# An adaLN transformer block on one core: softmax reciprocals moved from VectorE to GpSimd, and the last chunk's MLP weights requested round by round

## The chip, the cores and the metric

The kernel runs on one core of a Trainium2 chip. A core has a matrix engine (TensorE, "PE" in the profile, with its weight loads as "PEld"), VectorE ("DVE"), ScalarE ("ACT"), GpSimd ("POOL"), and SyncE ("SP"), which here only issues DMA transfers. Each engine works through its own list of instructions in order, and waits at semaphores for the others. The metric is the time of one execution in microseconds (us) on the device. The kernel before took 804.7 us, the median of 3 runs (804.57 to 805.7).

## The reference

The computation is one block with adaptive layer norm, self-attention and a bilinear gated MLP. The input x is (1, 2048, 640) in bf16; there are 32 heads of 20; the MLP's inner width is 1536.

```python
mod = (_silu(c) @ w_mod).reshape(1, 6, 1, -1)
sa, ca, ga, sb, cb, gb = (mod[:, i] for i in range(6))
h = layernorm(x) * (1 + ca) + sa
q, k, v = split_heads(h @ wqkv)                # 32 heads of 20
p = softmax(q @ k.T * 20 ** -0.5)              # 2048 x 2048 for each head
x = x + ga * ((p @ v) @ wo)
h = layernorm(x) * (1 + cb) + sb
x = x + gb * (((h @ w_gate) * (h @ w_up)) @ w_down)
```

## The kernel before, in words

**Order.** The file does not write out the order of its instructions. It describes every instruction as a task (class `Task`, line 39) with an engine, a planned duration, what it depends on, and a priority, and a list scheduler (class `Sched`, line 131) plays the whole program through once while the kernel is built. The order in which tasks start in that play is the order of each engine's list; `emit_program` (line 350) writes the lists with their semaphore waits. So a changed constant (`PE_SWITCH`, `PV_W`, `HAM_MIN`, `FILL_HARD`, or an entry of the table `STAGE`, which replaces such constants from a given item on) changes no computation, but may move any instruction. At run time nothing is rearranged: an engine that waits at one instruction also holds back all that stands behind it in its list. DMA transfers from SP have the same property: SP issues them one behind the other, in list order.

**Chunks and items.** The 2048 queries are taken in six chunks (512, 512, 256, 256, 256, 256). For a chunk, the 32 heads come in eight sets of four (`NSET`), and one set in one chunk is an item. For an item, PE computes transposed scores, four heads in the four 32-row strips of the array (line 1511), into PSUM; each group of scores fills two banks of it. ACT takes exp of the two banks at once (line 1548, 128x1024). Two pairs of banks alternate, so ACT can be at most a group behind PE. For a part of the groups' neighbours ("quads") DVE and POOL compute exp in place of ACT with integer operations: lines 1572, 1604 and 1612 on DVE, and a product that is either four quarter pieces on POOL (line 1624) or one whole operation on DVE (line 1609). PE then multiplies the exponentials with V (line 2177); V has a column of ones in front, so the same matmuls give the softmax denominators.

**End of an item** (`item_end_tasks`, line 1694). T1: DVE transposes the result out of PSUM into `OT` (line 1704). T2: DVE takes the reciprocals of the denominators into `invT` (line 1709). T3: `OTn` = `OT` times `invT` (line 1711), on POOL, or on DVE for the last set of heads of a chunk. T4: DVE transposes back into `OcT` (line 1720). Then four or five small DMA copies on SP move the rows into `Ocp` (line 1732), which the output projection reads.

**Behind each chunk** (`suffix`, line 1759). The output projection with its residual, the second layer norm (lines 1830 to 1837; its power of −1/2 is POOL's line 1835), transposes (line 1853 for the last chunk), twelve rounds of gate and up projection (one for each 128 of the 1536 columns), their product, the down projection, and the second residual (line 2047) are interleaved with the attention of the chunk that follows. Matmuls of this part are issued in quarters of the array (`quarters`, line 959, whose instruction is line 961); those of the last chunk, behind which no attention follows, use the whole array (`full`, line 957).

**MLP weights.** For each round, one load for gate and one for up (160 KB each, line 1917, on SP). Chunks before the last use the three buffers `stg` in turn: a pair can be asked for once the round three before it is done. The last chunk, number 5, finds ten of its twelve pairs in buffers of their own, `stx`, in which no other chunk's weights stand, and only its last two pairs go through `stg`. The dependency that decides from when on the `stx` pairs may be asked for stands in one expression:

```python
(sfx_done["qdead"] if fc < nsq else first)
    + oc_ready[(NC - 2, CHUNKS[-2][1] // 128 - 1)]   # if use_x
```

Here `fc` is the pair, `sfx_done["qdead"]` and `first` say when the memory that the buffers reuse is free, and `oc_ready[...]` are the `Ocp` copies of the last item of chunk 4.

Of the kernel before, what the change touches and what calls it, by code (L numbers as in the profile page):

```python
# [7 lines left out]
ALU = mybir.AluOpType  # L8
AX = mybir.AxisListType
BF16 = mybir.dt.bfloat16  # L10
F32 = mybir.dt.float32
# [1 line left out]

SEM = 60.0
PE_DRAIN = 170.0
PE_SWITCH = 102.0
PE_BACK = 112.0
PV_W = 219.0
X_FIRST = 0.0
ACT_LAT = 250.0  # L20
DVE_LAT = 40.0
# [10 lines left out]
STEAL_END = 66197.894  # L32
STEAL_GAP = 200
HAM_W = 3413.3
HAM_MIN = 2550.0
LKTOL = 300.0


# [311 lines left out]
def emit_program(nc, sched, nsem_dma=56):  # L350
# [123 lines left out]
CHUNKS = ((0, 512), (512, 512), (1024, 256), (1280, 256), (1536, 256), (1792, 256))  # L474
# [6 lines left out]
PV_KEEP = 2  # L481
# [10 lines left out]
EAGER = 7  # L492
# [3 lines left out]
XBACK = 0  # L496
HOLD = 110
PVTOL = 249
XDPRIO = 1.343
TPRIO = 0.75  # L500
TAHEAD = 1
GU_ONE = 1
XCONT = 0
T3_POOL = 1
HEAD_OUT = 2
NPS = 4
TS_4X, TT_2X = 600.0, 1145.0
# [23 lines left out]
PV0N = 1  # L531
GATE_F = (0.446, 0.6, 0.5, 0.5, 0.5, 1.0)
FILL_MIN = 4190.746
FILL_HARD = 3000.0
FILL_T0, FILL_TH, FILL_MINH = 2300.0, 17000.0, 7500.0
FILL_MODE = 'P'
DUP_MIN = 0.0
# [17 lines left out]
NTERM = 2  # L555

STAGE = {
    0: {"D_LATE": 16, "PVMIN": 2, "X_LATE": -179.96, "XDPRIO": 1.343, "LKTOL": 300.0, "FILL_MIN": 4190.746, "HOLD": 95, "TPRIO": 0.75, "PVTOL": 249, "EAGER": 9, "X_HALF": 0.0, "XBACK": 0, "D_RES": 74, "PVCAP": 12, "PVMAX": 14, "STEAL_GAP": 200, "PV_KEEP": 2},
    2: {"DL": 0.376},
    4: {"HOLD": 53.4},  # L560
    5: {"HOLD": 88.7, "STEAL_GAP": 176.5},
    7: {"DL": 0.501},
    9: {"LKTOL": 115.1},
    10: {"X_HALF": 5.8},
    11: {"DL": 0.443, "EAGER": 4, "FILL_MIN": 3731.3, "X_HALF": 38.6},
    12: {"DL": 0.459, "LKTOL": 438.4, "STEAL_GAP": 303.4, "EAGER": 10, "X_HALF": 21.8},
    13: {"DL": 0.417, "FILL_MIN": 4496.3, "STEAL_GAP": 266.2, "X_HALF": 20.9},
    15: {"LKTOL": 166.0, "PVMAX": 5, "EAGER": 10, "XBACK": 1},
    16: {"PVCAP": 10, "PVMAX": 3, "EAGER": 10, "FILL_MIN": 5086.4},
    17: {"X_HALF": -35.2},  # L570
    18: {"EAGER": 3, "X_LATE": -36.1, "HOLD": 42.4, "PVMIN": 1},
    19: {"DL": 0.471, "EAGER": 2, "X_HALF": 94.7},
    20: {"DL": 0.391},
    21: {"EAGER": 6, "FILL_MIN": 4510.3, "X_HALF": 24.2, "D_LATE": 5},
    22: {"PVMAX": 7, "X_HALF": 147.8, "EAGER": 9, "X_LATE": -21.9, "HOLD": 66.8},
    23: {"HOLD": 124.7, "X_HALF": 14.5},
    24: {"DL": 0.464},
    25: {"DL": 0.549, "PV_KEEP": 3, "X_LATE": 36.2},
    26: {"DL": 0.411, "X_LATE": 65.8, "PVMAX": 3, "EAGER": 8},
    27: {"DL": 0.473, "XBACK": 1, "HOLD": 186.0, "FILL_MIN": 3881.8, "X_LATE": -1.8},  # L580
    28: {"X_HALF": 33.6, "FILL_MIN": 4310.0, "XBACK": 0},
    29: {"PVMAX": 7, "X_LATE": -9.2},
    30: {"X_LATE": -109.9, "HOLD": 140.4, "XBACK": 1},
    31: {"X_LATE": 202.7, "D_RES": 21},
    32: {"PVCAP": 11, "X_HALF": -25.7, "X_LATE": 197.5},
    33: {"DL": 0.442},
    34: {"PVMIN": 5, "X_HALF": 27.8, "XBACK": 1},
    35: {"X_HALF": -31.6, "PVMAX": 14},
    36: {"DL": 0.524},
    37: {"X_LATE": -50.4},  # L590
    40: {"XBACK": 1, "HOLD": 36.3},
    41: {"X_LATE": 52.1, "X_HALF": -52.1},
    44: {"X_LATE": -66.5, "EAGER": 4, "D_RES": 10},
    47: {"FILL_MIN": 5302.0},
    48: {"PVCAP": 14, "FILL_MIN": 3192.3},
}
XHALF = 1
STG_G0, STG_G, XC_G = 12, -10, -20
# [12 lines left out]
def build_kernel(nc, A_x, A_wqkv, A_wo, B_x, B_w_gate, B_w_up, B_w_down, c, w_mod, out):  # L611
# [195 lines left out]
    def dve(dur, f, deps=(), prio=3.0, **k):  # L807
        return sc.add(Task("dve", dur, f, deps, prio=prio, **k))
# [73 lines left out]
    def load_rest():  # L882
# [5 lines left out]
        for q, f in enumerate((first2[0], first2[1],  # L888
# [690 lines left out]
    for qi, (it, us) in enumerate(dquads):  # L1579
# [36 lines left out]
        if X_POOL and qi % X_POOL == X_POOL - 1 and qi < len(dquads) - X_LAST and all(  # L1616
                dquads[z][0] == it for z in range(qi, min(len(dquads), qi + X_TAIL + 1))):
            st_["xby"] = None
            for x in range(X_PIECES):
                w = 2048 // X_PIECES  # L1620

                def fxp(e, x=x, w=w, st_=st_):
                    d = DSl[st_["ss"][0]][:, x * w:x * w + w].bitcast(BF16)
                    return e.tensor_tensor(d, DBl[st_["slot"]][:, x * w:x * w + w].bitcast(BF16), d, ALU.mult)  # L1624
                t = Task("pool", w * POOL_NS + 180.0, fxp, [tm, te], prio=2.0 + .1 * qi + .01 * x, name=f"XP.{qi}")
                t.lk = 2
                t.cond = lambda st_=st_: st_["xby"] != "dve"

                def on_p(task, x=x, st_=st_):
# [17 lines left out]
            def on_x(task, o0=o0, st_=st_):  # L1647
# [46 lines left out]
    def item_end_tasks(it):  # L1694
        ci, j = items[it]
        if ci == NC - 1 and j == 0:
# [12 lines left out]
        t2 = dve(155, lambda e: e.reciprocal(invT[:, 0:nb32].unsqueeze(2),  # L1709
                                            OT[:, 0:n].rearrange("p (b c) -> p b c", c=32)[:, :, 0:1]), [t1], prio=pe_)  # L1710
        f3 = lambda e: e.tensor_tensor(  # L1711
            OTn[:, 0:n].rearrange("p (b c r) -> p b r c", c=32, r=2),
            OT[:, 0:n].rearrange("p (b r c) -> p b r c", c=32, r=2),
            invT[:, 0:nb32].rearrange("p (b r) -> p b r", r=2).unsqueeze(3).to_broadcast([128, nb32 // 2, 2, 32]), ALU.mult)
        direct = j == NSET - 1 and ci == NC - 1
        if T3_POOL and not direct and not (END3 and j == NSET - 1):
            t3 = pool(n * 2.2 + 200, f3, [t2], prio=0)
        else:
            t3 = dvl(sb_cost(n, 1.04), f3, [t2], prio=pe_)
# [39 lines left out]
    def suffix(ci):  # L1759
# [148 lines left out]
        for fc in range(FT):  # L1908
            use_x = tail and fc < nsx
            wbuf, dm = [], []  # L1910
            for w_, wv in enumerate((wgv, wuv)):
                cell = {}
                if use_x:
                    cell["t"] = stx[fc][:, w_, :, :]

                def f(e, wv=wv, fc=fc, cell=cell):
                    return e.dma_start(cell["t"], wv[:, :, fc * 128:(fc + 1) * 128])
                t = dma("sp", int(STG_B * 128 * KD * 128 * 2), f,
                        (sfx_done["qdead"] if fc < nsq else first) + oc_ready[(NC - 2, CHUNKS[-2][1] // 128 - 1)] if use_x else
                        kp_use if ci == 0 else [], prio=16 + ci + .01 * fc,  # L1920
                        gate=int(gstart[NC] - 40) if tail and not use_x else 0 if tail else max(0, gb + (STG_G0 if ci == 0 else STG_G)))
                if not use_x:
                    t.acq = [(sStg[w_], "s", 1)]

                    def on0(task, cell=cell, w_=w_):
                        cell["i"] = task.slots["s"]
                        cell["t"] = stg[cell["i"]][:, w_, :, :]
                    t.on_start = on0
                wbuf.append(cell)
                dm.append(t)  # L1930
# [102 lines left out]
        for tl in range(ntl):  # L2033
# [5 lines left out]
            for (c_, w) in cuts:  # L2039
# [10 lines left out]
                if tail and TAILX:  # L2050
# [535 lines left out]
```

## Time and profile before

| what | us |
|---|---|
| median of 3 runs | 804.7 (804.57 to 805.7) |
| the profiled execution | 806.1 |
| its span, first to last instruction | 804.3 |
| PE busy | 786.4 |
| ACT busy, of it exps | 762.8, 746.8 |
| DVE busy | 688.5 |
| POOL busy | 361.9 |
| end of the last exp | 775.85 |

The profile is one execution of its own, with its own time. "Busy" is the time in which an engine executes something; busy times of engines overlap. In a row of groups the columns are: line of the kernel, engine, operation, tile written and tiles read, shape and type of each, count; then busy us and mean ns of one; then the idle time of the engine just ahead of such instructions and what ended it. In a row of a timeline they are: start in us from the span's start, duration of the run of like instructions in us, engine and line, operation, tiles, shape, count, and in brackets the idle time before it with its releaser. The releaser is inferred from semaphores: where an instruction waited for several things, the row names the one that seemed last, which can be wrong. A table by stretches gives busy us (and instructions) of PE, PEld, DVE, ACT and POOL, then the granted PE clock as a share of full speed, the busy share of the DMA engines, and GB/s.

### The profile page before, as it was taken

The page shows a single profiled execution, that of the slowest core. Times are in us where ns is not written, and L with a number is a line of the kernel's source. Part 1 is how long each engine was busy: PE and PEld are TensorE (multiplying, and loading weights), DVE is VectorE, ACT ScalarE, POOL GpSimd, SP SyncE. Part 2 cuts the span into 40 slices and gives each one's busy share as a digit, 9 for nine tenths or more (in the row PEclk, how much of TensorE's full clock was granted, in tenths as well). Part 3 has the DMA queues.
Part 4 walks back from the last instruction along what each step waited for, and adds up shares of the span by engine and source line. Part 5 has one row for each costly group of instructions (what it writes and reads, how often), then busy time and mean ns, then how long its engine had stood idle before and what let it go on. Part 6 is the DMA issues. An engine that isn't in the chain of part 4 may idle for free.

```text
span 804.3 us, 34189 instructions
## 1 busy us (share of the span) xinstructions
PE 786.4 (98%) x14875; PEld 345.9 (43%) x14875; DVE 688.5 (86%) x1355; ACT 762.8 (95%) x847; POOL 361.9 (45%) x373
## 2 busy tenths in 40 slices
PE   8999999999999999999999999999999999998998
PEld 4433423332233232323444444455555554544567
DVE  7989797898999899999877888988898989796654
ACT  6899899999999999999999999999999999998951
POOL 2443436545464643234664433654653434635400
PEclk9999999999999999999999999999999999999999
DMA  9843212202341522101301232100342054527400
GB/s 297 241 122 79 66 53 67 63 24 70 106 107 45 152 66 52 42 7 47 72 18 23 47 78 55 39 16 24 97 88 56 24 121 90 109 58 159 89 22 18
DMA packets 136387, 60.49 MB, mean 75 GB/s; under 512 B 100703, under 2 KB 136239, under 8 KB 136239
## 3 DMA queue, kind: packets, MB, share of 16 engines
q1 hardware_dynamic: 135311, 57.16, 28.0%
q8 instruction: 118, 1.93, 1.0%
q10 hardware_dynamic: 928, 1.15, 0.4%
q14 instruction: 30, 0.25, 0.1%
HBM read 46.70 MB, written 8.99 MB: 69 GB/s over the span
## 4 chain that ended last, share of the span: by engine, by line
PE 60%; ACT 24%; DVE 9%; issue 4%; DMA 2%; SPq 1%; ACTq 0%; DVEq 0%
ACT PP L1548 24%; PE ps_all L1511 20%; PE ps_all L961 18%; PE ps_all L2177 14%; DVE DB L1572 3%; PE ps_all L957 3%; PE ps_all L1221 2%; DMA wm<-in_w_mod_dram 1%; DVE DSS L1612 1%; DVE DSS L1604 1%; DVE DSS L1609 1%; SPq L1732 1%; PE ps_all L2510 1%; PE ps_all L1118 1%; PE ps_all L1157 1%
## 5 line engine op out<-in xcount | busy, mean ns | idle before, releaser
L1548 ACT ACTIVATE PP<-ps_all 128x1024 bf16<-128x1024 f32 x812 | 746.8, 1145 | 7.5 <-PE ps_all L1511 5.2
L1624 POOL TENSOR_TENSOR DSS<-DB,DSS 128x512 bf16<-128x512 bf16 x264 | 300.1, 1157 | 335.3 <-DVE DSS L1612 276.6
L1572 DVE TENSOR_SCALAR DB<-ps_all 128x512 int16<-128x512 f32 x424 | 283.6, 683 | 60.7 <-PE ps_all L1511 58.3
L1511 PE MATMUL ps_all<-QT,KT 32*128 32x256 bf16 (+2 forms) x3136 | 319.1, 307 | 7.0 <-ACT PP L1548 4.1
L1511 PEld LDWEIGHTS ps_all<-QT,KT 32*128 32x128 bf16 x3136 | 89.2, 92 | 229.2 <-ACT PP L1548 191.5
L2177 PE MATMUL ps_all<-PP,Vf 128*32 128x256 bf16 (+2 forms) x2504 | 164.0, 311 | 0.6 <-DVE Vf L1310 0.6
L961 PE MATMUL ps_all<-h2T,stg 128*32 128x256 bf16 (+2 forms) x2272 | 122.3, 303 | 0.8 <-DMA stg<-in_B_w_up_dram 0.5
L2177 PEld LDWEIGHTS ps_all<-PP,Vf 128*32 128x32 bf16 (+1 forms) x2504 | 50.2, 94 | 81.7 <-issue 74.7
L2177 PE MATMUL ps_all<-DSS,Vf 128*32 128x256 bf16 (+1 forms) x1264 | 84.9, 313 | 0.0
L1604 DVE TENSOR_SCALAR DSS<-DB 128x2048 int16<-128x2048 int16 x106 | 73.6, 695 | 0.6
L1612 DVE TENSOR_SCALAR DSS<-DB 128x2048 int16<-128x2048 int16 x106 | 73.1, 690 | 0.0
L961 PEld LDWEIGHTS ps_all<-h2T,stg 128*32 128x32 bf16 x2272 | 51.4, 96 | 30.2 <-issue 20.3
L961 PE MATMUL ps_all<-wd,hprod 128*32 128x320 bf16 (+1 forms) x1384 | 63.2, 279 | 0.0
L1711 POOL TENSOR_TENSOR OTn<-OT,invT 128x256 bf16<-128x256 f32 (+1 forms) x42 | 34.8, 829 | 34.2 <-DVE invT L1709 34.2
L1609 DVE TENSOR_TENSOR DSS<-DB,DSS 128x2048 bf16<-128x2048 bf16 x40 | 49.3, 1231 | 0.0
L2177 PEld LDWEIGHTS ps_all<-DSS,Vf 128*32 128x32 bf16 (+1 forms) x1264 | 31.3, 96 | 20.1 <-issue 8.5
L961 PEld LDWEIGHTS ps_all<-wd,hprod 128*32 128x32 bf16 x1384 | 31.0, 96 | 18.0 <-issue 12.2
L961 PE MATMUL ps_all<-wV,hT 128*32 128x160 bf16 x1280 | 37.6, 234 | 0.6 <-DVE DB L1572 0.2
L1221 PE MATMUL ps_all<-hT,wk 128*32 128x512 bf16 (+1 forms) x360 | 31.6, 382 | 0.4 <-DVE DB L1572 0.2
L1221 PE MATMUL ps_all<-hT,wq 128*32 128x512 bf16 x375 | 31.4, 382 | 0.0
L961 PEld LDWEIGHTS ps_all<-wV,hT 128*32 128x32 bf16 x1280 | 24.0, 96 | 15.4 <-issue 8.4
L961 PE MATMUL ps_all<-wo,Ocp 128*32 128x320 bf16 (+1 forms) x628 | 30.1, 287 | 0.0
(131 smaller groups left out, 525.5 us busy)
## 6 DMA issues: line engine op xcount, KB each, us to landing
stg<-in_B_w_gate_dram SPq DMA_DIRECT2D x62, 160.0 KB
stg<-in_B_w_up_dram SPq DMA_DIRECT2D x62, 160.0 KB
KT<-k_rows SPq DMA_DIRECT2D x112, 32.0 KB
wm<-in_w_mod_dram SPq DMA_DIRECT2D x3, 800.0 KB
x<-in_A_x_dram SPq DMA_DIRECT2D x7, 320.0 KB
k_rows<-KPA SPq DMA_DIRECT2D x16, 128.0 KB
QT<-q_rows SPq DMA_DIRECT2D x32, 64.0 KB
wd<-in_B_w_down_dram SPq DMA_DIRECT2D x1, 1920.0 KB
```

The costliest lines, as they stand in the source:

```text
L957: return lambda e, b: e.matmul(ps[:, b, c0:c0 + n], lhs(), rhs(), start=st, stop=sp)
L961: return lambda e, b: e.matmul(ps[32 * x:32 * x + 32, b, c0 + o:c0 + o + w], lhs()[:, 32 * x:32 * x + 32], rhs() if w == n else rhs()[:, o ...
L1221: f = [lambda e, b_, k=k, x=x: e.matmul(ps[x:x + min(32, w - x), b_, :], wx[:, k, r0 + x:r0 + min(x + 32, w)], hT[tc][:, k, :], tile_posit ...
L1511: ems.append(lambda e, i=i, kt=kt: e.matmul(dstf()[:, i * u.n:(i + 1) * u.n], KT[32 * u.s:32 * u.s + 32, u.j, kt * 128:(kt + 1) * 128], QT ...
L1548: return e.activation(PPs[g % 2][:, cellp["p"], 0:nu * 512], ps[:, b0:b0 + nu, :].rearrange("p b c -> p (b c)"), AFT.Exp, scale=ESCALE)
L1572: return e.tensor_scalar(DBl[st_["slot"]][:, x * 512:(x + 1) * 512], bank(cell["b"]), EBIAS, 0.0, op0=ALU.add, op1=ALU.max)
L1604: return e.tensor_scalar(DSl[st_["ss"][0]][:, :], DBl[st_["slot"]][:, :], 0x7F, 0x3F00, op0=ALU.bitwise_and, op1=ALU.bitwise_or)
L1609: return e.tensor_tensor(d, DBl[st_["slot"]][:, :].bitcast(BF16), d, ALU.mult)
L1612: return e.tensor_scalar(DSl[st_["ss"][1]][:, :], DBl[st_["slot"]][:, :], 0x7F80, 2, op0=ALU.bitwise_and, op1=ALU.bitwise_or)
L1624: return e.tensor_tensor(d, DBl[st_["slot"]][:, x * w:x * w + w].bitcast(BF16), d, ALU.mult)
L1711: f3 = lambda e: e.tensor_tensor(OTn[:, 0:n].rearrange("p (b c r) -> p b r c", c=32, r=2), OT[:, 0:n].rearrange("p (b r c) -> p b r c", c= ...
L2177: ems.append(lambda e, i=i, kt=kt, stt=stt, stp=stp: e.matmul(ps[32 * s:32 * s + mc, bk, 0:u.n], Vf[:, (kt * H + 4 * u.j + s) * VW:(kt * H ...
```

## The change

There are three parts. First, the reciprocal of the denominators (T2): for items whose T3 is on POOL, T2 moves to POOL too, as a power with exponent −1; a tile `mone` of −1 is filled once by POOL for it. Items whose T3 is on DVE keep their DVE reciprocal. Second, the loads into `stx` no longer wait for the `Ocp` copies of chunk 4's last item, but for the end of a round of chunk 4's gate and up projection: pair `fc` of the last chunk waits for round `fc // 2`. Third, four constants and the table `STAGE` are replaced, so the whole order is planned anew.

```diff
-PE_SWITCH = 102.0
+PE_SWITCH = 105.0
-PV_W = 219.0
+PV_W = 221.0
-HAM_MIN = 2550.0
+HAM_MIN = 3000.0
-FILL_HARD = 3000.0
+FILL_HARD = 3500.0
+T2_POOL, T2_NS = 1, 700.0
 STAGE = {
...
-    4: {"HOLD": 53.4},
-    5: {"HOLD": 88.7, "STEAL_GAP": 176.5},
+    3: {"D_LATE": 14, "PVMAX": 10, "PVTOL": 91.9},
+    4: {"PVMAX": 11},
+    6: {"PVMIN": 6, "STEAL_GAP": 183.1},
...
+    mone = alloc("mone", [128, 16], F32)
...
+    p_m1 = pool(100, lambda e: e.memset(mone[:], -1.0), prio=7)
...
-        t2 = dve(155, lambda e: e.reciprocal(invT[:, 0:nb32].unsqueeze(2),
-                                            OT[:, 0:n].rearrange("p (b c) -> p b c", c=32)[:, :, 0:1]), [t1], prio=pe_)
+        pooled = T3_POOL and not (j == NSET - 1 and ci == NC - 1) and not (END3 and j == NSET - 1)
+        dens = lambda: OT[:, 0:n].rearrange("p (b c) -> p b c", c=32)[:, :, 0:1]
+        if T2_POOL and pooled:
+            t2 = pool(T2_NS, lambda e: e.tensor_tensor(invT[:, 0:nb32].unsqueeze(2), dens(),
+                                                       mone[:, 0:nb32].unsqueeze(2), ALU.pow), [t1, p_m1], prio=0)
+        else:
+            t2 = dve(155, lambda e: e.reciprocal(invT[:, 0:nb32].unsqueeze(2), dens()), [t1], prio=pe_)
...
-        if T3_POOL and not direct and not (END3 and j == NSET - 1):
+        if pooled:
             t3 = pool(n * 2.2 + 200, f3, [t2], prio=0)
...
                 t = dma("sp", int(STG_B * 128 * KD * 128 * 2), f,
-                        (sfx_done["qdead"] if fc < nsq else first) + oc_ready[(NC - 2, CHUNKS[-2][1] // 128 - 1)] if use_x else
+                        (sfx_done["qdead"] if fc < nsq else first) + sfx_done["ulist"][fc // 2:fc // 2 + 1] if use_x else
...
+        sfx_done["ulist"] = u_last
```

Two further functions (`on_p`, `on_x`) get default arguments that they do not use.

More of the change, by code (lines that the diff above doesn't have):

```diff
@@ L557 @@
 STAGE = {
-    0: {"D_LATE": 16, "PVMIN": 2, "X_LATE": -179.96, "XDPRIO": 1.343, "LKTOL": 300.0, "FILL_MIN": 4190.746, "HOLD": 95, "TPRIO": 0.75, "PVTOL": 249, "EAGER": 9, "X_HALF": 0.0, "XBACK": 0, "D_RES": 74, "PVCAP": 12, "PVMAX": 14, "STEAL_GAP": 200, "PV_KEEP": 2},
-    2: {"DL": 0.376},
-    4: {"HOLD": 53.4},
-    5: {"HOLD": 88.7, "STEAL_GAP": 176.5},
-    7: {"DL": 0.501},
-    9: {"LKTOL": 115.1},
-    10: {"X_HALF": 5.8},
-    11: {"DL": 0.443, "EAGER": 4, "FILL_MIN": 3731.3, "X_HALF": 38.6},
@@ L566 @@
[L566 to L595, printed above, removed]
+    0: {"PVMIN": 2, "STEAL_GAP": 200, "XDPRIO": 1.343, "TPRIO": 0.75, "PVTOL": 249, "PVCAP": 12, "FILL_MIN": 4190.746, "PV_KEEP": 2, "X_HALF": 0.0, "D_RES": 74, "HOLD": 95, "D_LATE": 16, "X_LATE": -179.96, "PVMAX": 14, "LKTOL": 300.0, "EAGER": 9, "XBACK": 0},
@@ new lines @@
+    2: {"DL": 0.376, "XBACK": 4, "EAGER": 3},
+    3: {"D_LATE": 14, "PVMAX": 10, "PVTOL": 91.9},
+    4: {"PVMAX": 11},
+    6: {"PVMIN": 6, "STEAL_GAP": 183.1},
+    7: {"DL": 0.501},
+    8: {"X_HALF": -16.4},
+    9: {"LKTOL": 546.4, "XBACK": 0},
+    10: {"HOLD": 104.5, "PVMAX": 9, "PVTOL": 291.1},
+    11: {"DL": 0.443, "LKTOL": 386.6, "PVMAX": 8, "PVCAP": 9, "HOLD": 37.5},
+    12: {"DL": 0.459, "HOLD": 133.8},
+    13: {"DL": 0.417, "PVTOL": 88.1},
+    15: {"FILL_MIN": 4792.4, "D_LATE": 17, "PVMAX": 4},
@@ new lines @@
+    16: {"FILL_MIN": 4445.2},
+    17: {"STEAL_GAP": 312.2, "FILL_MIN": 5072.6, "D_RES": 17, "PVTOL": 185.7, "XBACK": 3},
+    19: {"DL": 0.471, "X_LATE": -75.5},
+    20: {"DL": 0.391, "HOLD": 117.9},
+    21: {"PVTOL": 224.1, "FILL_MIN": 5114.3},
+    22: {"PVTOL": 319.8},
+    23: {"D_RES": 35, "HOLD": 85.9},
+    24: {"DL": 0.464, "X_HALF": 87.9, "X_LATE": 34.6, "PVMIN": 1},
+    25: {"DL": 0.549, "PVMIN": 7, "PVTOL": 382.0, "HOLD": 103.9},
+    26: {"DL": 0.411, "X_HALF": -8.8, "X_LATE": 15.2, "PVMIN": 2},
@@ new lines @@
+    27: {"DL": 0.473, "EAGER": 5},
+    28: {"X_LATE": -63.9, "PVCAP": 11},
+    29: {"EAGER": 11, "LKTOL": 376.0},
+    31: {"LKTOL": 401.4, "X_LATE": -58.8, "HOLD": 114.3},
+    32: {"XBACK": 2, "X_LATE": -93.2},
+    33: {"DL": 0.442, "PV_KEEP": 1, "LKTOL": 261.2},
+    36: {"DL": 0.524, "PVTOL": 254.5, "X_LATE": -53.0},
+    38: {"FILL_MIN": 4567.2},
+    39: {"X_LATE": -98.7, "PVMAX": 8, "PVTOL": 316.5},
+    40: {"X_HALF": 49.3, "LKTOL": 383.9},
+    43: {"EAGER": 11, "X_HALF": 37.6},
+    44: {"X_HALF": -63.7},
@@ L596 @@
+    45: {"X_LATE": -90.4, "EAGER": 3},
+    46: {"HOLD": 91.2, "LKTOL": 47.3, "PVMIN": 2},
 }
@@ L1627, in build_kernel, with on_p @@
                 t.cond = lambda st_=st_: st_["xby"] != "dve"
-                def on_p(task, x=x, st_=st_):
+                def on_p(task, x=x, st_=st_, qi=qi, it=it, te=te):
                     if x == 0:
@@ L1645, in build_kernel, with on_x @@
             t.cond = lambda c0=c0, st_=st_: st_["xby"] is None and c0() and xjob[0] >= XBACK
-            def on_x(task, o0=o0, st_=st_):
+            def on_x(task, o0=o0, st_=st_, qi=qi, it=it, te=te):
                 o0(task)
```

## The prediction

> **What bounds the kernel now.** I read the page's busy shares, then the timeline of ACT, and beside each hole in it PE, SP and the clock.
>
> ```profile
> PE 786.4 (98%) x14875; PEld 345.9 (43%) x14875; DVE 688.5 (86%) x1355; ACT 762.8 (95%) x847; POOL 361.9 (45%) x373
> L1548 ACT ACTIVATE PP<-ps_all 128x1024 bf16<-128x1024 f32 x812 | 746.8, 1145 | 7.5 <-PE ps_all L1511 5.2
> ```
>
> The 812 exps are 746.8 us, 0.92 each. The first starts at 16.91 us, the last ends at 775.85, and from there to 804.3 PE works off the last chunk. So 16.9 and 28.5 us lie outside the exps and 758.9 inside, 12 more than the exps need; PE, 98% busy, has no slack to fill a hole with. One hole is worth a look (ACT's timeline; idle in brackets):
>
> ```profile
> 724.50 5.67 ACT L1548 ACTIVATE PP<-ps_all 128x1024 bf16<-128x1024 f32 x6
> 732.25 1.02 ACT L1548 ACTIVATE PP<-ps_all 128x1024 bf16<-128x1024 f32 x1 [2.07 <-PE ps_all L1511]
> 733.72 1.02 ACT L1548 ACTIVATE PP<-ps_all 128x1024 bf16<-128x1024 f32 x1 [0.45 <-PE ps_all L1511]
> 735.26 1.02 ACT L1548 ACTIVATE PP<-ps_all 128x1024 bf16<-128x1024 f32 x1 [0.51 <-PE ps_all L1511]
> 736.48 1.94 ACT L1548 ACTIVATE PP<-ps_all 128x1024 bf16<-128x1024 f32 x2 [0.20 <-PE ps_all L1511]
> ```
>
> Eleven exps take 738.42 − 724.50 = 13.92 us where 11 × 0.92 = 10.12 would do: 3.8 lost. PE's timeline says where it stood:
>
> ```profile
> 728.99 0.29 PE L961 MATMUL ps_all<-h2Tt,stg 128*32 128x256 bf16 x4
> 731.42 0.46 PE L961 MATMUL ps_all<-h2Tt,stg 128*32 128x256 bf16 x12 [2.14 <-DVE DSS L1612]
> ```
>
> The trace names DVE, but the waiting matmul reads a weight pair in `stg`, and SP's queue issued that pair late:
>
> ```profile
> 723.68 0.53 SPq L1917 DMA_DIRECT2D stx<-in_B_w_up_dram  x1
> ...
> 725.95 0.53 SPq L1917 DMA_DIRECT2D stg<-in_B_w_gate_dram  x1
> 726.53 0.56 SPq L1917 DMA_DIRECT2D stg<-in_B_w_up_dram  x1
> 727.13 2.03 SPq L1917 DMA_DIRECT2D stx<-in_B_w_up_dram  x1
> 731.72 3.80 SPq L1732 DMA_DIRECT2D Ocp<-OcT  x5
> ```
>
> Four loads of `stx` (weights of the last chunk, needed after 781) go ahead of the pair of round 4. The pair landed at 730.82 and 731.33 (DMA rows), and PE went on at 731.42. Behind the gap the clock fell (stretches of 4 us; PEclk third from the right):
>
> ```profile
> 728.00:732.00 4.00, 1.86 (x49) 1.04 (x46) 2.92 (x6) 2.17 (x3) 1.95 (x3) 1.00 0.93 183
> 732.00:736.00 4.00, 4.00 (x74) 2.09 (x70) 1.02 (x2) 2.79 (x3) 3.92 (x4) 0.57 0.60 121
> ```
>
> So of the 3.8 us about 2.1 are the wait and some 1.5 the half clock. Two smaller holes: exps 84.19 to 97.81 lose 2.6 us (twelve in 13.62; long runs of other matmuls and a 0.64 us wait for rows of Q), those around 54 us 0.9.
>
> **The change, part by part.**
>
> *1. Reciprocals.* Prices:
>
> ```profile
> L1609 DVE TENSOR_TENSOR DSS<-DB,DSS 128x2048 bf16<-128x2048 bf16 x40 | 49.3, 1231 | 0.0
> L1709 DVE RECIPROCAL invT<-OT 128x8 f32<-128x8 f32 x31 | 5.9, 192 | 0.2
> L1709 DVE RECIPROCAL invT<-OT 128x16 f32<-128x16 f32 x16 | 3.8, 240 | 0.0
> L1711 POOL TENSOR_TENSOR OTn<-OT,invT 128x256 bf16<-128x256 f32 x28 | 18.6, 665 | 25.5 <-DVE invT L1709 25.5
> L1711 POOL TENSOR_TENSOR OTn<-OT,invT 128x512 bf16<-128x512 f32 x14 | 16.2, 1155 | 8.7 <-DVE invT L1709 8.7
> L1835 POOL TENSOR_TENSOR rs<-sd,mhalf 128x1 f32<-128x1 f32 x16 | 9.8, 614 | 19.8 <-DVE sd L1833 19.0
> ```
>
> The 42 items whose L1711 is on POOL move; those of the last set of heads keep DVE. DVE loses 14 × 0.240 + 28 × 0.192 = 8.7 us. The new lists have 44 products on DVE instead of 40 (+4.9), so DVE nets −3.8 and POOL's quarter pieces fall from 264 to 248 (−16 × 1.157 = −18.5). POOL gains 42 powers. No power of 8 or 16 columns is in the trace. At one column a power is 0.55 to 0.61 us; L1711 grows by 1.9 ns a column. Low end: columns nearly free, 0.6. High end: all of the 0.25 us by which the power row exceeds a 128x1 tensor_scalar on POOL (0.35) is paid per column: 0.35 + 8 × 0.25 = 2.4, and 4.4 at 16. I take 0.6, the row of the same operation: 42 × 0.6 = +25, POOL +6.7 net of 362. Behind each power, on POOL, stand the item's L1711 and later pieces; on DVE its transpose L1720. POOL idles 335 us before its pieces, DVE 14% of the span, and those cover it. The new tile of −1 is one memset in the setup, where POOL has nothing to do. On the path: 0.
>
> *2. The loads.* Before, ten of the twenty `stx` loads are issued from 684 on and ten from 715 to 730. After, all wait for the end of a round of chunk 4's MLP, four for each of rounds 0 to 4. SP's new order behind the end of round 0: pair of round 3, 4 `stx`, pair 4, 4 `stx`, pair 5, 5 Ocp copies, pair 6, 6 `stx`, pair 7, 1 `stx`, 5 copies, pair 8, 3 `stx`, pair 9, 2 `stx`, pair 10. Pair 4 now has its four ahead of the end of round 1 that it waits for, so the wait at 729 goes: −3.8 with its half clock. What is late next? I count score groups at 0.91 us from the end of round 0. Round 8 starts at 25.5 us, round 9 at 28.2. SP at 0.57 a load (rows 723.68 to 726.53) and 0.76 a copy (3.80 / 5) reaches pair 8 at 23.5 and pair 9 at 26.4, and a pair lands 3 us after its second load's issue: PE waits 1.0 at round 8 and 0.2 more at round 9. Behind the waiting matmul stand PE's next scores, so ACT. Low price 1.2. But loads do not keep 0.57 for long: from 721.69 to 731.72 thirteen took 10.03 us, 0.77 each, and first bytes of loads in a row land 0.70 apart (DMA rows, 727.07 to 729.87 for five). If the ten loads ahead of round 8 go at 0.70, everything behind is 1.1 later: 2.3. [...] Bounds: 0, if SP is ahead, and some 5, if the waits fall into one and the clock halves.
>
> [...]
>
> *3. Everything else moved by the new constants.* The same 812 exps and the same matmul columns in new lists. The lists let me count work of PE between two runs of scores. Before, three stretches of 1.1 to 1.4 us early on; after, one of 2.8 us (40 of 128x320 and 52 of 128x160 by their rows, 37 and 22 ns each): ACT, one exp ahead, loses 2.0 in place of 2.6 + 0.9: −1.5. Bounds −3 and +2 (the Q rows, below). Four stretches of 0.9 to 1.0 us near the end are gone: −0.5. Then the tail:
>
> ```profile
> 779.70 1.54 PE L961 MATMUL ps_all<-wd,hprodt 128*32 128x320 bf16 x40
> 781.18 2.74 PE L957 MATMUL ps_all<-h2Tc,stx 128*128 128x128 bf16 x46
> ```
>
> PE is full here, and the down projection of chunk 4 left over behind the last scores grows from 48 to 108 matmuls (and 4 halves): 60 × 1.48 / 40 = +2.2. The second half's transposes now come after 9 instead of 46 MLP matmuls, and may wait for LN2: +0.3 (0 to 0.6).
>
> Sum: −3.8 + 1.5 − 1.5 − 0.5 + 2.2 + 0.3 + 0 = −1.8. It is made against the profiled execution, 806.1 (span 804.3 and 1.8 around it), which is 1.4 above the median of 804.7; nothing in the difference hangs on that, so I put it on the median: **802.9**.
>
> **Rivals.** (a) *SP takes the wait back.* The loads only move to other rounds. If they all stretch, the waits at rounds 7 to 9 are one of over 2 us with its half clock: 2.3 + 1.9 in place of 1.5, 805.6. For it: the 0.77. Against: six more rounds to spread over. (b) *Slower through the rows of Q.* In the lists Q's rows for the third set of heads are packed at unit 165 instead of 156 and needed at 178 instead of 176; the chain write, DMA, read back took 7.0 us before (83.92 to 90.9), and 13 units are 12 us, but five KT loads stand ahead on SP instead of four copies. It decides once the chain exceeds 12 us: at 14.0, twice as long, PE stands 2.0 more and, as at 729, loses 1.5 to the clock: 806.4. (c) *The power is dear.* At 2.4 to 4.4 us POOL gets 28 × 2.4 + 14 × 4.4 = 129 us instead of 25, and holds its pieces, the DVE transposes and the PV matmuls behind them: 104 us more, of which, POOL being busy 45% of its time, some 45% meets queued work: 845 and more. The order is written for 0.70 us a power, and L1711 takes 0.1 to 0.17 less than its constants in the code (763 and 1326 ns), so from about 0.85 us on it tells. (d) *The half clock is not the wait's.* The clock fell behind a gap of 2.14 us. If the halving came of the busy stretch around it, it comes again and the gain at 729 is 2.3: 804.4. The lists show that the loads and the reciprocals do move.
>
> [...]
>
> **How the numbers follow.** The forecast with better ones (its own range 800 to 804) 0.50; (a) 0.22, of which a quarter goes past 806.3; (d) 0.06; (b) 0.13; (c) 0.06; a wait that I see nowhere 0.03. A measurement here tells 0.2%, 1.6 us, from no change: 803.1 to 806.3 is "same". Faster: the forecast's 0.50, less 0.03 that lies above 803.1, 0.47. Same: 0.03 + 0.16 + 0.06 + 0.03 of (b)'s mild end = 0.28. Slower: 0.06 + 0.10 + 0.06 + 0.03 = 0.25. Range 799.6 (early holes 1.5 better, no wait at rounds 8 and 9, 1.5, transposes free, 0.3) to 807.0, which takes in (a) and the mild half of (b).
>
> **What would show it.** The POOL rows that write invT: under 0.85 us right, over 1.5 is (c). No PE gap over 1 us with `stg` near 729 and no PEclk under 1 behind it; gaps of 1 to 2 us in all at rounds 7 to 9. Early ACT holes summing to about 2; the last exp near 771.5, and a tail of 31 us instead of 28.5. Wrong: PEclk at half elsewhere, a wait for QT early, or POOL releasing PE.

## The result: slower, by 3.0%

The changed kernel takes 829.5 us, the median of 4 runs (822.78 to 832.5), against 804.63 for the kernel before in the same comparison. The ratio is 1.0298 with an interval of 1.0229 to 1.0368. The forecast was 802.9, range 799.6 to 807.0; it was wrong by its sign. The profiled execution took 832.5 us, with a span of 830.7; it is the slowest of the four, whose mean granted clocks go with their times (0.994 at 822.78 us, 0.992 at 827.37, 0.986 at 831.63, 0.985 at 832.5).

The page of the changed kernel, its busy shares and costliest groups (the line numbers shown are 2 to 8 higher than in the kernel before):

```profile
PE 796.2 (96%) x14819; PEld 346.9 (42%) x14819; DVE 704.1 (85%) x1317; ACT 767.6 (92%) x847; POOL 441.1 (53%) x400
...
L1550 ACT ACTIVATE PP<-ps_all 128x1024 bf16<-128x1024 f32 x812 | 751.3, 1093 | 24.9 <-PE ps_all L1513 20.9
...
L2185 PE MATMUL ps_all<-DSS,Vf 128*32 128x256 bf16 (+1 forms) x1264 | 85.9, 316 | 3.8 <-POOL DSS L1626 3.4
...
L1606 DVE TENSOR_SCALAR DSS<-DB 128x2048 int16<-128x2048 int16 x106 | 80.5, 760 | 0.4
L1614 DVE TENSOR_SCALAR DSS<-DB 128x2048 int16<-128x2048 int16 x106 | 79.0, 745 | 0.6 <-PE ps_all L2185 0.5
...
L1611 DVE TENSOR_TENSOR DSS<-DB,DSS 128x2048 bf16<-128x2048 bf16 x44 | 57.1, 1299 | 0.1
```

Three things stand out. The idle time of ACT ahead of its exps went from 7.5 to 24.9 us, 20.9 of it ended by the scores (line 1513). POOL is 79 us busier, where +7 was reckoned. DVE lost 42 reciprocals and is yet 16 us busier: its products (line 1611) take 7.8 us more, where +4.9 was reckoned, and the same 106 operations of lines 1606 and 1614 (1604 and 1612 before) went from 695 and 690 ns to 760 and 745. The groups of POOL, with shapes apart, give the power's price:

```profile
L1714 POOL TENSOR_TENSOR invT<-OT,mone 128x8 f32<-128x8 f32 x28 | 48.0, 1713 | 53.7 <-DVE OT L1706 53.7
L1714 POOL TENSOR_TENSOR invT<-OT,mone 128x16 f32<-128x16 f32 x14 | 43.6, 3112 | 24.5 <-DVE OT L1706 24.4
```

A power of 8 columns is 1.71 us and one of 16 is 3.11: 0.175 us a column on 0.31. The DVE reciprocals that they replace were 0.19 and 0.24.

To see where the time lies I laid the starts of the 812 exps against 0.905 us apiece (the spacing that recurs where nothing waits) and summed what lies above, in us, by exps. The other columns are experiments told below; all come from one profiled execution each.

| exps | before | changed | multiplied | half powers | old loads | multiplied, old loads |
|---|---|---|---|---|---|---|
| first exp starts at | 16.9 | 19.1 | 15.8 | 15.8 | 15.8 | 16.2 |
| 0 to 54 | 6.4 | 5.8 | 7.1 | 5.8 | 6.0 | 6.0 |
| 54 to 108 | 3.0 | 6.1 | 5.7 | 4.2 | 6.1 | 6.5 |
| 108 to 216 | 1.3 | 3.8 | 1.3 | 1.3 | 3.8 | 1.3 |
| 216 to 243 | 0.3 | 6.1 | 0.3 | 0.5 | 1.1 | 0.4 |
| 243 to 702 | 7.2 | 10.1 | 6.3 | 7.9 | 10.1 | 6.5 |
| 702 to 756 | 0.6 | 5.2 | 0.8 | 1.1 | 2.7 | 0.7 |
| 756 to the end | 5.1 | 8.7 | 8.5 | 9.8 | 9.5 | 2.5 |
| behind the last exp | 28.5 | 30.7 | 30.7 | 30.8 | 31.3 | 31.3 |

The loss is not one hole. Some of it is many small holes all along, some is in the row of exps 756 on, where chunk 4's MLP runs. And some belongs to this one execution: the late first exp and the rows 216 to 243 and 702 to 756 hold stretches of half clock (3.41 us from 11.21, 6.83 from 239.90 and from 724.60) that the run with the old loads, whose engines have the same lists up to there, does not have (experiment 2). One of the small holes, whole. POOL's timeline in the changed kernel:

```profile
106.89 2.91 POOL L1714 TENSOR_TENSOR invT<-OT,mone 128x16 f32<-128x16 f32 x1
109.76 1.64 POOL L1626 TENSOR_TENSOR DSS<-DB,DSS 128x512 bf16<-128x512 bf16 x1
111.36 1.50 POOL L1718 TENSOR_TENSOR OTn<-OT,invT 128x512 bf16<-128x512 f32 x1
112.82 1.15 POOL L1626 TENSOR_TENSOR DSS<-DB,DSS 128x512 bf16<-128x512 bf16 x1
```

DVE beside it, then PE and ACT behind it:

```profile
110.30 1.65 DVE L1614 TENSOR_SCALAR DSS<-DB 128x2048 int16<-128x2048 int16 x1
```

```profile
114.02 0.40 PE L2185 MATMUL ps_all<-DSS,Vf 128*32 128x512 bf16 x4 [1.21 <-POOL DSS L1626]
```

```profile
114.99 5.66 ACT L1550 ACTIVATE PP<-ps_all 128x1024 bf16<-128x1024 f32 x6 [1.03 <-PE ps_all L1513]
```

Behind the power, on POOL, stand a quarter piece of an exp product, the item's line 1718 and a second piece. The first piece, late by the power, and DVE's line 1614 run into each other: 1.64 in place of 1.16 us, and 1.65 in place of 0.68. The second piece ends at 113.97; PE, in order, had stood 1.21 us for it, and ACT 1.03. Nothing on POOL was idle for long, but a chain that ended just in time now ended late. With a multiplication in the power's place (experiment 1) the same list goes:

```profile
105.80 0.22 POOL L1714 TENSOR_TENSOR invT<-OT,mone 128x16 f32<-128x16 f32 x1
105.98 1.15 POOL L1626 TENSOR_TENSOR DSS<-DB,DSS 128x512 bf16<-128x512 bf16 x1
107.10 1.05 POOL L1718 TENSOR_TENSOR OTn<-OT,invT 128x512 bf16<-128x512 f32 x1
109.96 1.15 POOL L1626 TENSOR_TENSOR DSS<-DB,DSS 128x512 bf16<-128x512 bf16 x1 [1.82 <-DVE DSS L1614]
```

There POOL waits 1.82 us for DVE, and PE and ACT have no such hole. Over the whole changed kernel PE waits 3.4 us for POOL's pieces and 3.3 for DVE's line 1574, against 0 and 0.5 before: the holes come by way of a late DVE as much as straight from POOL.

What DVE loses beside POOL depends on what runs there: in the changed kernel line 1614 takes 681 ns on average where no POOL instruction runs (68 of them) and 967 where a quarter piece or line 1718, and no power, runs for part of it (24). Beside a power it takes no longer: nine of line 1614 ran beside one for at least four fifths of their time and took 685 (the other five beside one for a shorter part, 654). So the powers do not lengthen this DVE operation directly; they shift large POOL pieces into it.

The end of the attention stretch is the second place. PE's timeline, and ACT's:

```profile
767.04 0.51 PE L963 MATMUL ps_all<-h2Tt,stg 128*32 128x256 bf16 x12 [2.79 <-DMA stg<-in_B_w_up_dram]
773.41 1.15 PE L963 MATMUL ps_all<-h2Tt,stg 128*32 128x256 bf16 x20 [2.98 <-DMA stg<-in_B_w_up_dram]
```

```profile
767.91 3.77 ACT L1550 ACTIVATE PP<-ps_all 128x1024 bf16<-128x1024 f32 x4 [2.61 <-PE ps_all L1513]
775.14 1.02 ACT L1550 ACTIVATE PP<-ps_all 128x1024 bf16<-128x1024 f32 x1 [3.45 <-PE ps_all L1513]
776.78 1.02 ACT L1550 ACTIVATE PP<-ps_all 128x1024 bf16<-128x1024 f32 x1 [0.62 <-PE ps_all L1513]
778.30 1.02 ACT L1550 ACTIVATE PP<-ps_all 128x1024 bf16<-128x1024 f32 x1 [0.49 <-PE ps_all L1513]
```

The wait at 729 us of the kernel before is gone, and two longer ones stand in its place; behind the second the clock is halved (exps 1.5 us apart, PEclk 0.55 and 0.60 in the 4 us stretches from 772). SP's queue shows why:

```profile
761.10 0.53 SPq L1924 DMA_DIRECT2D stx<-in_B_w_up_dram  x1
761.66 0.53 SPq L1924 DMA_DIRECT2D stg<-in_B_w_gate_dram  x1
762.24 1.85 SPq L1924 DMA_DIRECT2D stg<-in_B_w_up_dram  x1
764.13 0.77 SPq L1924 DMA_DIRECT2D stx<-in_B_w_gate_dram  x1
764.94 3.52 SPq L1739 DMA_DIRECT2D Ocp<-OcT  x5
768.50 0.58 SPq L1924 DMA_DIRECT2D stg<-in_B_w_gate_dram  x1
769.12 0.52 SPq L1924 DMA_DIRECT2D stg<-in_B_w_up_dram  x1
```

The pair of round 7 is asked for at 761.66, behind six `stx` loads; its second half, asked for at 762.24, landed at 767.0. The pair of round 8 comes behind five copies at 768.50 and 769.12 and landed at 773.3 (times of landing from the trace's semaphore events). SP was hardly idle from 742.97 to 776.4: fourteen loads from 742.97 to 753.0 took 0.72 us each.

### The profile page after: what moved, and what is told of

Its sections match the earlier page's. It is cut to its first block, busy times and chain, and to the rows that moved or that the text cites. A ratio compares the mean times of both kernels' runs of the same rounds, so it can differ in the third digit from the quotient of the medians.

```text
span 830.7 us, 34048 instructions
## 1 busy us (share of the span) xinstructions
PE 796.2 (96%) x14819; PEld 346.9 (42%) x14819; DVE 704.1 (85%) x1317; ACT 767.6 (92%) x847; POOL 441.1 (53%) x400
## 4 chain that ended last, share of the span: by engine, by line
PE 56%; DVE 19%; ACT 13%; POOL 5%; issue 4%; DMA 2%; SPq 1%; DVEq 0%; ACTq 0%
PE ps_all L1513 19%; PE ps_all L963 15%; PE ps_all L2185 13%; ACT PP L1550 13%; DVE DB L1574 7%; PE ps_all L1223 3%; PE ps_all L959 3%; DVE DSS L1606 3%; DVE DSS L1614 3%; POOL invT L1714 2%; POOL DSS L1626 2%; DVE DSS L1611 2%; DMA wm<-in_w_mod_dram 1%; POOL OTn L1718 1%; PE ps_all L1120 1%
## 5 line engine op out<-in xcount | busy, mean ns | idle before, releaser
L1550 ACT ACTIVATE PP<-ps_all 128x1024 bf16<-128x1024 f32 x812 | 751.3, 1093 | 24.9 <-PE ps_all L1513 20.9
L1626 POOL TENSOR_TENSOR DSS<-DB,DSS 128x512 bf16<-128x512 bf16 x248 | 284.4, 1163 | 236.5 <-DVE DSS L1614 178.0
L1714 POOL TENSOR_TENSOR invT<-OT,mone 128x8 f32<-128x8 f32 (+1 forms) x42 | 91.5, 2179 | 78.2 <-DVE OT L1706 78.1
L2185 PEld LDWEIGHTS ps_all<-PP,Vf 128*32 128x32 bf16 x2504 | 48.9, 94 | 82.2 <-issue 73.0
L1606 DVE TENSOR_SCALAR DSS<-DB 128x2048 int16<-128x2048 int16 x106 | 80.5, 760 | 0.4
L1614 DVE TENSOR_SCALAR DSS<-DB 128x2048 int16<-128x2048 int16 x106 | 79.0, 745 | 0.6 <-PE ps_all L2185 0.5
L1611 DVE TENSOR_TENSOR DSS<-DB,DSS 128x2048 bf16<-128x2048 bf16 x44 | 57.1, 1299 | 0.1
L1718 POOL TENSOR_TENSOR OTn<-OT,invT 128x256 bf16<-128x256 f32 (+1 forms) x42 | 39.2, 934 | 2.0
L1706 DVE STREAM_TRANSPOSE OT<-ps_all 128x256 f32<-128x256 f32 (+2 forms) x49 | 25.6, 523 | 9.7 <-PE ps_all L2185 9.6
L1223 PE MATMUL ps_all<-hT,wk 128*32 128x512 bf16 x360 | 32.5, 382 | 0.4 <-DVE Vf L1312 0.2
```

Source lines behind the costliest of these rows:

```text
L1223: f = [lambda e, b_, k=k, x=x: e.matmul(ps[x:x + min(32, w - x), b_, :], wx[:, k, r0 + x:r0 + min(x + 32, w)], hT[tc][:, k, :], tile_posit ...
L1550: return e.activation(PPs[g % 2][:, cellp["p"], 0:nu * 512], ps[:, b0:b0 + nu, :].rearrange("p b c -> p (b c)"), AFT.Exp, scale=ESCALE)
L1606: return e.tensor_scalar(DSl[st_["ss"][0]][:, :], DBl[st_["slot"]][:, :], 0x7F, 0x3F00, op0=ALU.bitwise_and, op1=ALU.bitwise_or)
L1611: return e.tensor_tensor(d, DBl[st_["slot"]][:, :].bitcast(BF16), d, ALU.mult)
L1614: return e.tensor_scalar(DSl[st_["ss"][1]][:, :], DBl[st_["slot"]][:, :], 0x7F80, 2, op0=ALU.bitwise_and, op1=ALU.bitwise_or)
L1714: t2 = pool(T2_NS, lambda e: e.tensor_tensor(invT[:, 0:nb32].unsqueeze(2), dens(), mone[:, 0:nb32].unsqueeze(2), ALU.pow), [t1, p_m1], prio=0)
```

## The experiments

Theory A: the length of the powers makes most of the loss. Theory B: the loads and the new order do. All ratios are to the kernel before on the same chip; the medians of the first four belong to 806.52 us of the kernel before, of the next four to 805.02, of the last two to 807.5.

**1. Powers replaced by multiplications, everything else in its place.** The inversion of the denominators is left out.

```diff
-                mone[:, 0:nb32].unsqueeze(2), ALU.pow)
+                mone[:, 0:nb32].unsqueeze(2), ALU.mult)
```

> The changed kernel with each of its 42 powers replaced by a multiplication of the same shape on the same engine, at the same place of the same lists (so the softmax denominators multiply by -1 instead of being inverted: the arithmetic of that step is left out, everything else is as in the changed kernel). Theory A, the length of the powers (1.64 us at 8 columns and 2.91 at 16, where the order was written for 0.70) makes most of the loss: the multiplication takes about 0.3 to 0.45 us, the scattered losses of the stretch go, the two waits for weights near the end stay with their half clock (7.5 us), and the time is 808 to 813. Theory B, the loads and the new order make it: nothing but a few us of POOL time changes, and the time stays at 822 or more.

813.55 us, 1.0085 (1.0056 to 1.0113). The multiplications:

```profile
L1714 POOL TENSOR_TENSOR invT<-OT,mone 128x8 f32<-128x8 f32 x28 | 7.2, 257 | 54.9 <-DVE OT L1706 54.9
L1714 POOL TENSOR_TENSOR invT<-OT,mone 128x16 f32<-128x16 f32 x14 | 5.1, 366 | 24.6 <-DVE OT L1706 24.4
```

The time is half a us above theory A's range and far from theory B's. All lists are those of the changed kernel, so 1.0298 − 1.0085 = 2.1%, some 17 us, goes with the powers' length (the values computed behind them differ too, which no run separates). The two intervals leave 1.2 to 3.1%, and experiments 2 and 5, the same pair of kernels with the old loads, give 1.4%. DVE's lines 1606 and 1614 are back at 697 and 691 ns. In the table the holes of exps 108 to 216 vanish and those of 702 to 756 nearly (for 216 to 243 see experiment 2); those of the row 756 on stay, as theory A had it.

**2. The old dependency of the loads in the changed kernel.**

```diff
-   ... + sfx_done["ulist"][fc // 2:fc // 2 + 1] if use_x else
+   ... + oc_ready[(NC - 2, CHUNKS[-2][1] // 128 - 1)] if use_x else
```

> The changed kernel with the old dependency of the last chunk's loads; the lists differ only from chunk 4's MLP on. Theory A: the powers stay, the two waits of 2.8 and 3.0 us for weights go, with their half clock 7.5 us, and a wait like that at 729 us of the kernel before may come back (0 to 4): 820 to 827. Theory B: with the loads out of the way most of the loss is gone, 810 or less.

822.86 us, 1.0202 (1.0169 to 1.0235): 1% better than the changed kernel and within A's 820 to 827. But the two intervals overlap, and the changed kernel's fastest run took 822.78 us, so the 1% is not clear of noise. The row of exps 756 on stays at 9.5. There is one wait in place of two, 3.18 us for a pair asked for behind nine `stx` loads, and the clock is halved behind it (exps 1.5 us apart, PEclk 0.50 from 748 to 752):

```profile
749.14 1.02 ACT L1550 ACTIVATE PP<-ps_all 128x1024 bf16<-128x1024 f32 x1 [3.74 <-PE ps_all L1513]
750.67 1.02 ACT L1550 ACTIVATE PP<-ps_all 128x1024 bf16<-128x1024 f32 x1 [0.50 <-PE ps_all L1513]
752.18 1.02 ACT L1550 ACTIVATE PP<-ps_all 128x1024 bf16<-128x1024 f32 x1 [0.49 <-PE ps_all L1513]
```

The profile's gain over the changed kernel's is in other rows: 3.3 us at the start, 5.0 in exps 216 to 243, where the changed kernel's execution had a 2.7 us wait of DVE for a DMA (`KPB` waiting for `q_rows`) with a half clock behind it (PEclk 0.50 and 0.66 in the 4 us stretches from 240), and 2.5 in exps 702 to 756, where in the changed kernel's execution the clock halves behind a gap of no more than 0.8 us:

```profile
720.00:724.00 4.00, 3.23 (x61) 1.37 (x56) 3.80 (x7) 3.48 (x5) 2.89 (x3) 1.00 0.00 0
724.00:728.00 4.00, 4.00 (x59) 1.61 (x60) 3.23 (x9) 3.02 (x4) 2.14 (x2) 0.57 0.15 50
```

Up to there the lists of PE, ACT, DVE and POOL are the same in both kernels, and SP's are for the first two rows. So those two are differences between executions and no effect of the edit, and the third is most likely one as well; what the loads are worth has to be read from the medians.

**3. Reciprocals on VectorE, the rest of the change kept.**

```diff
-T2_POOL, T2_NS = 1, 700.0
+T2_POOL, T2_NS = 0, 700.0
```

> The changed kernel planned with the reciprocals on VectorE (constants and loads as in the change; the planner orders everything anew). Theory A: no powers, so no scattered losses; loads in bursts of four to eight between the MLP's weight pairs may still make PE wait once or twice: 804 to 812, the power rows are gone from POOL and DVE's 128x2048 rows are back near 0.69 us. Theory B or a fault of the new constants: 820 or more.

838.85 us, 1.0401 (1.0349 to 1.0453): slower still, which neither theory expected. The attention stretch is 775.8 us, 5 shorter than the changed kernel's, but behind the last exp lie 42.6 us in place of 30.7. The new list explains it: 132 gate and up matmuls and 192 down matmuls of chunk 4 stand behind the last scores, where the changed kernel has 112 down matmuls. So this run doesn't tell A from B. It shows that the table `STAGE` fits one plan: taking a part away lets the planner make another order, and the comparison is then between two orders.

**4. The new dependency alone, in the kernel before.**

```diff
-   ... + oc_ready[(NC - 2, CHUNKS[-2][1] // 128 - 1)] if use_x else
+   ... + sfx_done["ulist"][fc // 2:fc // 2 + 1] if use_x else
...
+        sfx_done["ulist"] = u_last
```

> The kernel before with the new dependency of the loads alone. My prediction's reckoning (the wait at 729 us goes, waits of 1 to 2 us come at later rounds): 801 to 804. Rival, the loads stretch to 0.72 us each and SP is never free from round 0 to round 9: waits of 3 to 6 us in all with a half clock, 806 to 811.

810.46 us, 1.0059 (1.0035 to 1.0084), as the rival had it. Few rows of PE's and DVE's lists move. In its profile PE waits 3.8 us for `stg` in two places, 3.0 in the longer, at a mean granted clock of 0.998 over the span; exps 756 on lose 7.9 in place of 5.1, and 29.7 us lie behind the last exp in place of 28.5. My reckoning of 801 to 804 falls.

**5. Multiplications and old loads together.** Both edits, in the changed kernel; what is left is the new order.

```diff
-                mone[:, 0:nb32].unsqueeze(2), ALU.pow)
+                mone[:, 0:nb32].unsqueeze(2), ALU.mult)
...
-   ... + sfx_done["ulist"][fc // 2:fc // 2 + 1] if use_x else
+   ... + oc_ready[(NC - 2, CHUNKS[-2][1] // 128 - 1)] if use_x else
```

> The changed kernel with both suspects undone at once: the powers replaced by multiplications of the same shape (the inversion of the denominators is left out) and the old dependency of the loads. What is left of the change is the new order. If the two costs add (16.0 us for the powers, 6.6 for the loads, from the first four runs), 806.9, so within 2.5 us of the kernel before: the new order by itself brings nothing. If the new order is a gain of its own, as my reckoning of the early holes had it, 802 to 804. If the two overlap in the same waits, 810 or more.

811.67 us, 1.0062 (1.0032 to 1.0091), ten runs from 806.62 to 814.74. The new order by itself is no gain but a loss of some 5 us. Much of that is half clock: four of the ten runs took 806.6 to 808.4 at a mean granted clock of 0.998, six 811.2 to 814.7 at 0.989 to 0.994. With the old loads the powers cost 1.0202 − 1.0062 = 1.4%, some 11 us, in place of 2.1%; with multiplications, undoing the loads brings 0.2% (1.0085 to 1.0062), with powers 1%. So the time is in the range given for costs that overlap, but 1.4 and 2.1% lie within each other's intervals, and whether the costs add stays open. The profiled execution is one of the faster ones: it has 3.5 us more in exps 54 to 108 (with a half clock at 96 us, PEclk 0.63 from 96 to 100) and 2.8 behind the last exp than the kernel before, and 2.6 less in the row 756 on.

**6. Half of each power, in the changed kernel.** The power is taken on half the columns, and line 1718 multiplies by `mone`; the inversion is left out.

```diff
-  invT[:, 0:nb32] ... dens() ... mone[:, 0:nb32] ... ALU.pow
+  invT[:, 0:nb32 // 2] ... dens()[:, 0:nb32 // 2] ... mone[:, 0:nb32 // 2] ... ALU.pow
```

> The changed kernel, same lists, with each power taken on the first half of its columns only (4 or 8), and L1718 multiplying by the tile of -1, so that no half is read unwritten (the inversion is left out). From 0.37 us and 0.16 a column a power is then about 1.0 us or 1.64. If every us of power above the multiplication's length costs alike, the loss of 16.0 us falls to 0.49 of it: 821 (820 to 823). If only what exceeds the planned 0.70 to 0.85 us costs, 15.3 us of excess are left of 55.7: 818 (816 to 819).

814.94 us, 1.0110 (1.0070 to 1.0150), below what both reckonings expected.

```profile
L1714 POOL TENSOR_TENSOR invT<-OT,mone 128x4 f32<-128x4 f32 x28 | 29.7, 1061 | 54.7 <-DVE OT L1706 54.7
L1714 POOL TENSOR_TENSOR invT<-OT,mone 128x8 f32<-128x8 f32 x14 | 25.1, 1793 | 24.5 <-DVE OT L1706 24.3
```

42 us more on POOL than with the multiplications cost some 2 us (0.25%, inside the intervals); the next 37 us, to the full powers, cost 15. So the loss is no fixed share of POOL's time: powers of 1.1 us in the short items and 1.8 in the long ones cost little, and most of the loss comes between these and the full 1.7 and 3.1. Where in between it sets in, and at how many of the 42 items, is not measured.

**7. Ten loads as before, the other ten spread over rounds 1, 3, 5, 7 and 9, in the kernel before.**

```diff
-   ... + oc_ready[(NC - 2, CHUNKS[-2][1] // 128 - 1)] if use_x else
+   ... + (oc_ready[(NC - 2, CHUNKS[-2][1] // 128 - 1)] if fc < 5 else sfx_done["ulist"][2 * fc - 9:2 * fc - 8]) if use_x else
```

> The kernel before, with the first ten of the last chunk's loads as they were (behind the copies, some 684 us) and the other ten asked for one pair behind each second round of chunk 4's MLP (rounds 1, 3, 5, 7, 9). The lists of all engines but SP stay as before. Theory: the wait at 729 us goes with its half clock, nothing is late in its place: 3.8 us less than before. If the half clock comes of something else, 2.3 less. If SP has no room in the rounds either, the wait comes back later: no gain or a loss.

803.16 us, 0.9970 (0.9945 to 0.9995). Only SP's list differs. ACT where the kernel before stood 2.07 us:

```profile
720.99 24.11 ACT L1548 ACTIVATE PP<-ps_all 128x1024 bf16<-128x1024 f32 x26
```

Twenty-six exps without a gap, and PEclk 1.00 in all five stretches from 726 to 746: wait and half clock went together in this execution. Exps 756 on lose 1.6 here, 5.1 before. The medians cannot tell the expected 3.8 us from the 2.3 of the other reading: they differ by 1.9, and the interval reaches from 0.4 to 4.4. This execution lost 3.6 us at its start to a half clock there (exps 1.5 us apart from 21.79 to 24.82), which the kernel before had not.

**8. The planner told the power's real length.**

```diff
-            t2 = pool(T2_NS, ...
+            t2 = pool(350 + 160 * nb32, ...
```

> The changed kernel with the planned length of the power set to what the chip takes (350 ns and 160 a column in place of 700); the order is planned anew. If the loss comes of an order that does not know the power's length, most of the 16 us comes back: 812 to 820. If POOL's time and its collisions with DVE cost by themselves, 824 or more. Planning anew may shift either by some us, as the run with the reciprocals on VectorE showed.

852.17 us, 1.0571 (1.0525 to 1.0617). The stretch is 775.3 us, 5.7 shorter than the changed kernel's, but 58.7 us lie behind the last exp: 440 gate and up matmuls of chunk 4 were left there. As in 3, another order, whose tail costs more than a known length saves. Whether a table made for the true length would pay stays open; it was not tried.

**9. All twenty loads, one pair behind each round, in the kernel before.**

```diff
+   ... + sfx_done["ulist"][fc:fc + 1] if use_x else
```

> The kernel before with all twenty loads asked for one pair behind each round (pair fc behind round fc); the lists of DVE, ACT and POOL stay as before, PE's differ in a few rows, SP's order changes. A round lasts 3.6 us; SP then has four loads and about 1.05 us of copies in each. If loads keep 0.57 us (my prediction's low price), that is 3.3, SP keeps up, and the time is that of the run with ten loads spread, 802 to 804. If loads go at 0.72 in the long run, as in the changed kernel (fourteen in 10.07 us from 742.97 on), it is 3.9, SP falls behind by 0.3 us a round, and waits of 1 to 3 us with a half clock come late in the MLP: 806 to 811, as with the changed kernel's dependency alone.

802.94 us, 0.9943 (0.9922 to 0.9964). The time is the one expected if SP keeps up, but the profile is not so clean: its execution, at the slow end of the ten (802.12 to 805.03), has a wait of 2.9 us for `stg` with a half clock (the next exps start 1.42 and 1.52 us apart).

```profile
738.56 1.02 ACT L1548 ACTIVATE PP<-ps_all 128x1024 bf16<-128x1024 f32 x1 [2.75 <-PE ps_all L1511]
```

Whether the faster executions have it too isn't seen. Against experiment 4, which differs in bunching alone (four loads a round over five rounds, against two over ten), it is 1.2% faster by the ratios, though the two did not run side by side.

**10. The powers alone, in the kernel before.**

> The kernel before with the powers alone (planned at 0.70 us), old constants, old loads; the planner orders everything anew. The new list leaves 124 gate and up matmuls and 192 down matmuls of chunk 4 behind the last scores, where the kernel before has 48 down matmuls: by 0.037 us for a 128x320 and about 0.03 for a 128x256 quarter some 9 us of tail, 37 to 41 us instead of 28.5. To that comes what the powers cost in the attention stretch, 10 to 15 us: 822 to 832. If the powers are cheap where the order was not made for the change's constants, 812 to 816.

Three runs took 830.19 to 833.01 us, 1.0302 (1.0259 to 1.0344), at the upper end of what was expected. The profiled execution is a fourth and took 852.81, so only the price is read from it: 1.76 and 3.09 us a power, much as before. This kernel, too, is planned anew with a longer tail, so how much of the 24 us is the powers and how much the tail is not separated here.

## Why the prediction was wrong, point by point

*The power's price* is the step that failed: 0.6 us a power, covered, so 0 on the path, where the runs show 1.71 and 3.11 us and 1.4 to 2.1% of the time (11 to 17 us). Of the rest of the 3.0%, the new order by itself has 0.6% (experiment 5) and the loads 0.2 to 1.0%, by whether the powers are taken out first. The prediction bounded the price at 0.6 us from below and 2.4 and 4.4 us from above, and took "0.6, the row of the same operation". That row has one column. It fixes an offset and says nothing of a slope, and the shape at hand had 8 and 16. The measured slope, 0.175 us a column, is seven tenths of the upper end's 0.25. Rival (c) named this mechanism with 0.06; it deserved more, since of the two ends only the upper one used the excess that the row showed. Its own price (845) was too high: powers longer than the 0.85 us that I read from the order still cost little (experiment 6), and only 11 to 17 us came of it.

*The cover* ("POOL idles 335 us, DVE 14% of the span") was a sum over the span. What was needed was the slack of the pieces next behind each power. By experiment 6 it nearly covers 1.1 us in the short items and 1.8 in the long ones, and not the full powers. The wait of 1.21 us at 114.02, behind a power of 16 columns, is such a piece.

*The loads.* The wait at 729 was read rightly, with its cause, though the profile named DVE: spread the loads and it is gone (experiment 7), and the half clock with it, which speaks against rival (d) at this place, by one execution; in the changed kernel the clock also halved at 725 us without such a wait (experiment 2). What came next was put at rounds 8 and 9 and mis-sized: no run shows the 1.5 us that the sum takes for it, between the reckoned 1.2 and 2.3; the changed kernel waits 2.79 and 2.98 us at rounds 7 and 8, with a half clock (PEclk 0.55 and 0.60 in the 4 us stretches from 772). Its ACT rows sum to 2.61 + 3.45 + 0.62 + 0.49, 7.2 us, above the stated bound of 5. Two terms fail. One is the 0.57 us a load: fourteen in a row ran at 0.72. The other is the 3 us from a pair's second request to its landing: it was 4.8 at round 7 and 4.2 at round 8, and the rows that the forecast read at 729 already had 4.8 (726.53 to 731.33), beside 3.0 for the pair before (723.11 to 726.12). Also, ten loads at 0.13 more make 1.3, not 1.1. Rival (a) had the pace, with 0.22. The new dependency alone makes the kernel 0.6% slower (experiment 4).

*The new order.* Early holes were put at 2.0 in place of 3.5. The long stretch of other matmuls that I counted is there and costs 2.5 in each of the five profiled executions of this order, but other holes of 1 to 3 us lie around it, so exps 0 to 108 lose 10 to 13 us in place of 9.4: no gain. The tail was right: +2.2 and +0.3 forecast, and 30.7 to 31.3 measured in place of 28.5. Rival (b)'s place, the rows of Q, shows no wait of PE for them there.

## What to carry to other kernels

A price taken from a row of another shape needs a slope: take the end of the range that has one, or measure. Idle time summed over a span covers nothing by itself; ask how late the very next user of that engine's output may be. And transfers that nobody waits for still belong ahead of, or evenly between, those that somebody does: with the same twenty loads, four a round cost 0.6% and two a round gained 0.6%.

## What the runs showed of the hardware

The clock halves behind some gaps and not behind others of like length. Halved: 2.14 us (before, at 729, PEclk 0.57 from 732 to 736), 2.98 (changed, at 773, PEclk 0.55 from 772 to 776), 3.18 (old loads, at 747, PEclk 0.50 from 748 to 752). Not halved: 2.79 (changed, at 767, PEclk 1.00 from 764 to 772) and this one, of experiment 5 (PEclk 1.00 from 736 to 744), after which fourteen exps run at full pace in ACT's timeline:

```profile
738.23 0.73 PE L963 MATMUL ps_all<-h2Tt,stg 128*32 128x256 bf16 x20 [2.11 <-DMA stg<-in_B_w_up_dram]
```

So a wait of 2 to 3 us costs itself, or itself and more: 1.5 us before, at 729, and at least 2.5 with the old loads, where five exps from 749.14 to 755.23 start 1.52 us apart in place of 0.905. The times scatter with it: the ten runs of experiment 5 lie 8 us apart. How long the half clock lasted differs too. By the clock records it was 3.41 us before, from 732.36, and in the changed kernel 3.41 from 11.21 and 6.83 from each of 239.90, 724.60 and 772.38; the run with the old loads was at half clock for some 13 us in all, an estimate from its mean granted clock of 0.992 over 821.3 us. The length of PE's idle time alone does not decide it: 2.79 us halved nothing, and from 718 us to the half clock at 724.60 of the changed kernel PE was idle for 0.77 us in all. What does decide no run here shows.
